# One more unit step between scores, turn and values in the attention loop of an attention and mixture-of-experts kernel

## The chip, the cores and the metric

The kernel runs on one core of one Trainium2 chip. The metric is the device time of one execution in microseconds. Three runs of the kernel before took 601.81, 603.10 and 607.35 us; their median is 603.1 us.

## The reference

Attention over q, k and v of shape (batch 8, heads 8, sequence 576, head dimension 64), all float32, and then a mixture of experts over the 4608 tokens of width 512 that the heads make together.

```python
rel = pos[:, None] - pos[None, :]
mask_local = (rel >= 0) & (rel < 32)
mask_strided = (rel >= 0) & (pos[None, :] % 32 == pos[:, None] % 32)
# heads 0 to 3 are local, heads 4 to 7 strided
scores = np.where(mask, scale * q @ k.T, -1e9)
attn = softmax(scores)              # denominator + 1e-09
x = (attn @ v), heads side by side  # 4608 x 512
logits = x @ w_gate + modality_bias[modality_id]
e_idx = argmax(logits); gate = softmax(logits)[e_idx]   # 8 experts
out = gate * (relu(x @ w1[e_idx]) @ w2[e_idx])          # 512 -> 1024 -> 512
```

## The kernel before, in words

**Two stages.** In the attention stage, up to about 165 us of the trace, the heads are computed and each token is routed to an expert. In the feed-forward stage that follows, 18 slots of 256 tokens of one expert each and a half slot of 128 tokens run one after the other, in three matmuls for each product (the float32 operands are split into a high and a low part).

**Units and steps.** The attention work is cut into 32 units, local and strided in turn. A local unit is one local head of two batches, a strided unit two strided heads of one batch. Eight units make a pair of batches. Each unit goes through `load` (queries and keys), `prep` (local only, copies of the queries into a block form), `masks` and `scores`, `load_values`, `turn` and `values`. The loop over `n` (lines 1050 to 1093) is a software pipeline: in step n it issues the scores of unit n, the turn of unit n-2 and the values of unit n-3. So in a local step (n even) the scores and the turn are of local units and the values of a strided one; in a strided step the other way round.

**What a unit computes.** `scores` multiplies queries and keys into two PSUM banks on TensorE (for a local unit L346, the tile `s`; for a strided one L442, `ss`), takes the maximum and the difference on VectorE (L353 and L354; L454 and L455) and the exponential on ScalarE (L355 and L356, tile `ex`; L456, tile `exs`). A strided unit is normalised here already: sum, +1e-9, reciprocal and product on VectorE (L458 to L462) give `en`. `turn` transposes on TensorE (the helper's line 227, tiles `t` and `ts`) and copies out of PSUM on ScalarE (L368 and L371 into `et`; L471 into `eb`). `values` multiplies by the values (L382 and L388, tile `o`; L483, tile `ot`). A local unit's result is normalised on VectorE (L392 to L398) into the rows `xt`, a strided unit's is copied on ScalarE (L491) into the columns `xc`.

**Buffers.** All PSUM tiles come from one pool of eight banks, used in turn; a step's masks, turn and values take two each. `ex` has two buffers (the pool's default) and `en` two fixed buffers that the units use in turn, with zeros in the last ten columns that GpSimd writes once at the start (L300). `et` has one buffer, the loaded tiles two.

**Order.** The order on TensorE is the program's (a manual schedule for that engine alone). The instructions of VectorE, ScalarE and GpSimd are put in order by a planner that simulates the program; those inside `pin` keep the program's order. The loads go out on SP's queue in program order. From step 3 on they are paced: the first half of the queries and keys of unit n+3 waits for the last values matmul, the second half for the last scores matmul, and the two parts of the values of unit n-1 for the last turn and the last values matmul (`follow`, L242). FILL puts matmuls on zeros ahead of the masks of steps 2 and 3.

**What hangs on the last values of a pair.** When the eighth unit's values are issued, a generator (`after`, L995) joins a list; every step takes five pieces from it. They turn the local rows into columns (tile `xl`), multiply by the gate weights (`lg`), turn the strided columns into rows (`xs`), rank the tokens by expert and, after the second, third and fourth pair, build the tables of slots. The rows are stored to memory by one DMA in each step on GpSimd's queue (`store_rows`). At steps nu-4, nu-3 and nu-2 (28, 29 and 30) the loop looks up, gathers and starts to load for the first two slots or halves of weights; at step nu+1 it turns the first slot's tokens. What is left of the last pair's list is done inside the first feed-forward slots.

Of the kernel before, what the change touches and what calls it, by code (L numbers as in the profile page):

```python
# [11 lines left out]
F32 = mybir.dt.float32  # L12
# [8 lines left out]
P = 128  # L21
# [170 lines left out]
def attention_moe(ctx: ExitStack, tc: tile.TileContext, a, out):  # L192
# [31 lines left out]
    at = {"scores": None, "turn": None, "values": None}  # L224
# [63 lines left out]
    lp = lp_cm.__enter__()  # L288


    def zeros(n, shape, name):
        return [lp.tile(shape, F32, bufs=1, name=f"{name}{i}") for i in range(n)]

    qds = zeros(2, [P, 18, 2, 32], "qd")
    ets = zeros(1, [P, 18, 2, 32], "et")
    ens = zeros(2, [P, 12, 64], "en")
    for t in qds + ets:
# [5 lines left out]
    class Local:  # L303
# [34 lines left out]
        def scores(self):  # L338
            n, qk, qd = self.n, self.qk, self.qd
            mx = lp.tile([P, 9], F32, tag="mx", name=f"mx{n}")  # L340
            self.ex = ex = lp.tile([P, 11, 64], F32, tag="ex", name=f"ex{n}")
            for g0, gn, s in self.ss:
# [60 lines left out]
    class Strided:  # L403
# [30 lines left out]
        def scores(self):  # L434
# [25 lines left out]
            nc.vector.reciprocal(sm[:], sm[:])  # L460
            self.en = ens[n % 2]
            nc.vector.tensor_tensor(self.en[:, :, 0:54], ex[:], bc(sm, 12), ALU.mult)  # L462
# [532 lines left out]
    def after(bp, xt, xcs):  # L995
        yield from finish_pair(bp, xt, xcs)
        yield
        for ph, (last_bp, _) in enumerate(PHASES):
            if bp == last_bp:
                yield from slots(ph)  # L1000
# [48 lines left out]
    man.__enter__()  # L1049
    for n in range(nu + 3):  # L1050
        paced = n >= PACED

        if not paced:
            for part in range(2):
                if n + 3 < nu:
                    units[n + 3].load(part, None)
            for part in range(2):
                if 1 <= n <= nu:
                    units[n - 1].load_values(part, None)
        if n in FILL:  # L1060
# [6 lines left out]
        if paced and n + 3 < nu:  # L1067
            units[n + 3].load(1, at["scores"])
        if 2 <= n <= nu + 1:
            units[n - 2].turn()  # L1070
        if paced and n <= nu:
            units[n - 1].load_values(0, at["turn"])
        if n >= 3:
            units[n - 3].values()
            if n - 3 in ends:
                extra.append(after(*ends[n - 3]))
        if paced and n <= nu:
            units[n - 1].load_values(1, at["values"])
        if n == SETUP:
# [5 lines left out]
        for i in range(2):  # L1085
# [4 lines left out]
            if n == nu - 2:  # L1090
                load(0, i)
        if n == nu + 1:
            turn(0)
# [70 lines left out]
```

## Time and profile before

| | before |
|---|---|
| median of three runs | 603.1 us (601.81 to 607.35) |
| profiled execution | 602.83 us |
| span of its trace | 601.0 us |
| TensorE busy | 565.7 us (94%) |
| VectorE busy | 446.8 us (74%) |
| ScalarE busy | 388.6 us (65%) |
| GpSimd busy | 250.4 us (42%) |
| granted clock of TensorE, mean | 0.993 |

The trace is of one execution. Its span starts with the first instruction and ends with the last; the run's time is 1.8 us longer. PE is TensorE, PEld its weight loads, DVE VectorE, ACT ScalarE, POOL GpSimd, SP the engine on whose queue the loads go out. A share of busy time over the whole span is a mean over the two stages, which differ: the feed-forward stage is two and a half times as long as the attention stage. "x<-y" names the tile written and the tiles read. A number in brackets after an instruction is the engine's idle time before it and what ended it; "issue" is idle time in which the engine waited for nothing that the profile shows. The clock is given as a share of full speed.

### The profile page before, as it was taken

How to read it: one execution, taken by the hardware profiler on the slowest of the kernel's cores; microseconds unless marked ns; L12 is line 12 of the kernel's file. 1: busy time of each engine (PE TensorE's matmuls, PEld its weight loads, DVE VectorE, ACT ScalarE, POOL GpSimd, SP SyncE). 2: the span in 40 equal slices, each digit the busy share in tenths (PEclk: the TensorE clock that was granted, in tenths of full speed). 3: DMA queues.
4: the chain of work that ended last, by engine and by line, in shares of the span. 5: the costliest groups of instructions: out<-in, count | busy, mean ns of one | idle time of the engine just before them, and what ended most of it. 6: DMA issues, size and time to landing. Idle time of an engine off the chain costs nothing.

```text
span 601.0 us, 15492 instructions
## 1 busy us (share of the span) xinstructions
PE 565.7 (94%) x6107; PEld 498.5 (83%) x6109; DVE 446.8 (74%) x1076; ACT 388.6 (65%) x798; POOL 250.4 (42%) x226
## 2 busy tenths in 40 slices
PE   8777899797899999999999999999999999999995
PEld 4666787676669999999999999999999999999994
DVE  7867886985968799666787787787787787787542
ACT  4767877765796666776665575575665665665652
POOL 0011011117237537555645645645645646532310
PEclk9999899999999999999999999999999999999998
DMA  8984997998844944744754743313214239413621
GB/s 311 299 259 152 335 316 257 322 306 273 267 115 164 219 168 105 217 170 106 177 210 106 219 167 93 71 36 105 72 37 106 70 116 277 111 40 72 228 103 41
DMA packets 73572, 102.46 MB, mean 170 GB/s; under 512 B 48531, under 2 KB 48787, under 8 KB 69908
## 3 DMA queue, kind: packets, MB, share of 16 engines
q0 software_dynamic: 20672, 58.01, 28.6%
q1 hardware_dynamic: 52340, 42.87, 26.8%
q8 instruction: 50, 0.82, 0.6%
q10 hardware_dynamic: 480, 0.51, 0.3%
q14 instruction: 30, 0.25, 0.1%
HBM read 123.85 MB, written 19.18 MB: 238 GB/s over the span
## 4 chain that ended last, share of the span: by engine, by line
PE 82%; ACT 7%; DVE 6%; issue 3%; POOL 0%; another core or an unknown queue 0%; POOLq 0%; ACTq 0%
PE h L940 34%; PE o L954 33%; PE o L382 2%; PE s L346 2%; PE ot L483 1%; ACT xc L491 1%; PE lg L543 1%; PE xs L227 1%; PE ts L227 1%; DVE ex L354 1%; DVE mx L353 1%; DVE sms L458 1%; PE t L227 1%; PE warm L212 1%; ACT et L368 1%
## 5 line engine op out<-in xcount | busy, mean ns | idle before, releaser
L976 DVE TENSOR_TENSOR wl<-raw,wh 128x512 fp32r<-128x512 f32 x288 | 187.7, 691 | 64.2 <-ACT wh L975 55.2
L975 ACT CAST wh<-raw 128x512 fp32r<-128x512 f32 x288 | 163.9, 619 | 66.6 <-PE o L954 43.1
L940 PE MATMUL h<-xh,wl 128*128 128x256 f32 x576 | 162.7, 283 | 0.0
L940 PE MATMUL h<-xl,wh 128*128 128x256 f32 x576 | 162.6, 283 | 0.0
L940 PE MATMUL h<-xh,wh 128*128 128x256 f32 x576 | 162.4, 282 | 0.1
L822 POOL DMA_INDIRECT raw<-in_w,wi x72 | 95.9, 1332 | 156.3 <-DVE wl L976 117.6
L940 PEld LDWEIGHTS h<-xh,wh 128*128 128x128 f32 x576 | 109.5, 190 | 7.5 <-issue 0.6
L940 PEld LDWEIGHTS h<-xl,wh 128*128 128x128 f32 x576 | 109.6, 190 | 5.5
L954 PE MATMUL o<-wh,hh 128*128 128x512 f32 x288 | 114.2, 396 | 0.0
L954 PE MATMUL o<-wl,hh 128*128 128x512 f32 x288 | 113.8, 395 | 0.0
L940 PEld LDWEIGHTS h<-xh,wl 128*128 128x128 f32 x576 | 109.7, 190 | 1.4 <-DVE wl L976 0.4
L954 PE MATMUL o<-wh,hl 128*128 128x512 f32 x288 | 110.5, 391 | 0.0
L943 ACT ACTIVATE hh<-h 128x256 fp32r<-128x256 f32 x144 | 55.4, 385 | 71.1 <-PE h L940 46.7
L945 DVE SCALAR_TENSOR_TENSOR hl<-h,hh 128x256 fp32r<-128x256 f32 x144 | 60.7, 421 | 33.3 <-ACT hh L943 21.6
L954 PEld LDWEIGHTS o<-wh,hl 128*128 128x128 f32 x288 | 53.5, 188 | 11.0
L954 PEld LDWEIGHTS o<-wh,hh 128*128 128x128 f32 x288 | 54.6, 189 | 7.6
L954 PEld LDWEIGHTS o<-wl,hh 128*128 128x128 f32 x288 | 54.6, 190 | 5.6
L962 POOL DMA_INDIRECT out<-y,le x36 | 44.7, 1242 | 20.6 <-ACT y L961 11.0
L806 POOL DMA_INDIRECT fx<-xd,le x36 | 40.1, 1113 | 11.9 <-issue 10.7
L813 POOL DMA_INDIRECT le<-ld,li x36 | 39.4, 1095 | 12.9 <-issue 10.1
L498 POOL DMA_DIRECT2D xd<-xt x20 | 14.5, 727 | 62.3 <-ACT xt L507 62.3
L382 PE MATMUL o<-vv,et 128*64 128x65 f32 x512 | 22.7, 231 | 5.5 <-issue 3.3
(189 smaller groups left out, 749.1 us busy)
## 6 DMA issues: line engine op xcount, KB each, us to landing
vv<-in_vl SPq DMA_DIRECT2D x32, 292.5 KB
qks<-in_qks SPq DMA_DIRECT2D x32, 288.0 KB
xd<-xt POOLq DMA_DIRECT2D x16, 512.0 KB
qk<-in_qkl SPq DMA_DIRECT2D x16, 304.0 KB
qk<-in_qkl SPq DMA_DIRECT2D x16, 288.0 KB
vs<-in_vs SPq DMA_DIRECT2D x32, 144.0 KB
raw<-in_w,wi POOLq DMA_INDIRECT x72
xd<-xt POOLq DMA_DIRECT2D x4, 256.0 KB
```

The source lines that it names most:

```text
L227: at["turn"] = nc.tensor.transpose(dst, src, ident)
L382: at["values"] = nc.tensor.matmul(o[64 * jj:64 * jj + 64, k, :], et[:, u, :, :].rearrange("p g q -> p (g q)"), vv[:, u, :], start=True, st ...
L806: pin(nc.gpsimd.indirect_dma_start(xt[:, h, :], None, xd[0:xrows, :], IOA(ap=le[:, h, 0:1], axis=0)))
L813: pin(nc.gpsimd.indirect_dma_start(le[:, h, :], None, ld[0:xrows, :], IOA(ap=li[:, s, h:h + 1], axis=0)))
L822: pin(nc.gpsimd.indirect_dma_start(raws[j].rearrange("p f c -> p (f c)"), None, a["w"], IOA(ap=wi[:, s, j:j + 1], axis=0), bounds_check=E ...
L940: nc.tensor.matmul(hp, w[:, a1], x[:, c, :], start=(k == 0), stop=(k == 11))
L943: nc.scalar.activation(hh[:], hp, AF.Relu)
L945: nc.vector.scalar_tensor_tensor(hl[:], hp, 0.0, hh.bitcast(F32), ALU.max, ALU.subtract)
L954: nc.tensor.matmul(os[h], hx[:, m], w[:, 512:1024], start=(f == 0 and i == 0), stop=(f == 7 and i == 2))
L962: outs.add(pin(nc.gpsimd.indirect_dma_start(out, IOA(ap=le[:, h, 0:1], axis=0), y[:], None, bounds_check=NT - 1, oob_is_err=False)))
L975: nc.scalar.copy(wh[:, c], raw[:, c])
L976: nc.vector.tensor_tensor(wl[:, c], raw[:, c], wh[:, c].bitcast(F32), ALU.subtract)
```

## The change

The turn of a unit is issued three steps behind its scores and its values four steps behind, in place of two and three. The value loads go out two steps behind the scores in place of one. The loop has one more pass, 36 in place of 35, and the list of a pair starts with the values of its last unit, so one step later. The steps at which slots are looked up, gathered and loaded keep their numbers; the turning of the first slot's tokens keeps its distance from the end. `ex` and `en` get a third buffer. Since the lag between scores and turn is now odd, a local step has local scores, a strided turn and local values, and a strided step has strided scores, a local turn and strided values.

```diff
--- before.py
+++ after.py
@@ -293,7 +293,7 @@
 
     qds = zeros(2, [P, 18, 2, 32], "qd")
     ets = zeros(1, [P, 18, 2, 32], "et")
-    ens = zeros(2, [P, 12, 64], "en")
+    ens = zeros(3, [P, 12, 64], "en")
     for t in qds + ets:
         nc.vector.memset(t[:], 0.0)
     for t in ens:
@@ -338,7 +338,7 @@
         def scores(self):
             n, qk, qd = self.n, self.qk, self.qd
             mx = lp.tile([P, 9], F32, tag="mx", name=f"mx{n}")
-            self.ex = ex = lp.tile([P, 11, 64], F32, tag="ex", name=f"ex{n}")
+            self.ex = ex = lp.tile([P, 11, 64], F32, tag="ex", bufs=3, name=f"ex{n}")
             for g0, gn, s in self.ss:
                 for g in range(gn):
                     for jj in range(2):
@@ -458,7 +458,7 @@
             nc.vector.tensor_reduce(sm[:], ex[:], AX.X, ALU.add)
             nc.vector.tensor_scalar(sm[:], sm[:], 1e-9, None, ALU.add)
             nc.vector.reciprocal(sm[:], sm[:])
-            self.en = ens[n % 2]
+            self.en = ens[n % 3]
             nc.vector.tensor_tensor(self.en[:, :, 0:54], ex[:], bc(sm, 12), ALU.mult)
 
         def turn(self):
@@ -1047,7 +1047,7 @@
             units[i].prep()
     man = tc.manual_schedule(engines={mybir.EngineType.PE})
     man.__enter__()
-    for n in range(nu + 3):
+    for n in range(nu + 4):
         paced = n >= PACED
 
         if not paced:
@@ -1055,8 +1055,8 @@
                 if n + 3 < nu:
                     units[n + 3].load(part, None)
             for part in range(2):
-                if 1 <= n <= nu:
-                    units[n - 1].load_values(part, None)
+                if 2 <= n <= nu + 1:
+                    units[n - 2].load_values(part, None)
         if n in FILL:
             keep_busy(FILL[n], f"warm{n}")
         if paced and n + 3 < nu:
@@ -1066,16 +1066,16 @@
             units[n].scores()
         if paced and n + 3 < nu:
             units[n + 3].load(1, at["scores"])
-        if 2 <= n <= nu + 1:
-            units[n - 2].turn()
-        if paced and n <= nu:
-            units[n - 1].load_values(0, at["turn"])
-        if n >= 3:
-            units[n - 3].values()
-            if n - 3 in ends:
-                extra.append(after(*ends[n - 3]))
-        if paced and n <= nu:
-            units[n - 1].load_values(1, at["values"])
+        if 3 <= n <= nu + 2:
+            units[n - 3].turn()
+        if paced and n <= nu + 1:
+            units[n - 2].load_values(0, at["turn"])
+        if n >= 4:
+            units[n - 4].values()
+            if n - 4 in ends:
+                extra.append(after(*ends[n - 4]))
+        if paced and n <= nu + 1:
+            units[n - 2].load_values(1, at["values"])
         if n == SETUP:
             routing_setup()
         if n + 2 < nu:
@@ -1089,7 +1089,7 @@
                 gather(i)
             if n == nu - 2:
                 load(0, i)
-        if n == nu + 1:
+        if n == nu + 2:
             turn(0)
     man.__exit__(None, None, None)
     lp_cm.__exit__(None, None, None)
```

## Rows read from the trace of the kernel before

**Rows 1.** Busy time by stage: stretch, length, us (instructions) per engine, clock, DMA, GB/s.

```profile
0.00:17.00 17.00, 14.48 (x232) 8.58 (x236) 12.97 (x29) 8.56 (x18) 0.54 (x6) 1.00 0.88 298
17.00:60.00 43.00, 33.48 (x901) 28.16 (x901) 31.39 (x85) 29.50 (x66) 4.33 (x8) 1.00 0.75 238
60.00:100.00 40.00, 36.02 (x956) 31.11 (x948) 31.64 (x105) 31.56 (x73) 4.83 (x8) 0.96 0.91 295
100.00:140.00 40.00, 32.88 (x810) 27.46 (x799) 33.25 (x133) 29.06 (x66) 9.52 (x11) 1.00 0.97 326
140.00:165.00 25.00, 20.19 (x472) 16.78 (x472) 20.01 (x85) 15.15 (x35) 11.14 (x14) 1.00 0.77 250
165.00:601.00 436.00, 428.68 (x2777) 386.40 (x2775) 317.53 (x642) 274.78 (x545) 220.07 (x181) 0.99 0.45 129
```

**Rows 2.** Waits of TensorE, 17 to 165 us: total us, times, longest.

```profile
PE ts L227 <- DVE en L462: 6.2, 5, 1.9
PE ot L483 <- issue: 3.6, 6, 0.9
PE o L382 <- issue: 3.3, 3, 2.3
PE xl L227 <- DVE xt L398: 1.9, 1, 1.9
PE o L382 <- ACT xc L514: 1.5, 2, 0.9
PE ot L483 <- ACT et L368: 1.3, 1, 1.3
PE ss L431 <- DVE xt L398: 1.0, 1, 1.0
```

**Rows 3.** Timeline of TensorE, turns that waited: start, us, what, [idle before].

```profile
22.53 0.85 PE L227 MATMUL ts<-cf_sb,en 128*128 128x128 f32 x6 [1.22 <-DVE en L462]
30.37 0.85 PE L227 MATMUL ts<-cf_sb,en 128*128 128x128 f32 x6 [1.94 <-DVE en L462]
71.22 1.54 PE L227 MATMUL ts<-cf_sb,en 128*128 128x128 f32 x6 [0.89 <-DVE en L462]
108.90 0.88 PE L227 MATMUL ts<-cf_sb,en 128*128 128x128 f32 x6 [1.47 <-DVE en L462]
152.57 0.87 PE L227 MATMUL ts<-cf_sb,en 128*128 128x128 f32 x6 [0.69 <-DVE en L462]
```

**Rows 4.** Busy time in one microsecond of the same kernel, columns as in group 1.

```profile
71.00:72.00 1.00, 0.78 (x4) 0.78 (x5) 0.97 (x8) 0.98 (x3) 0.00 (x0) 0.50 1.11 268
```

**Rows 5.** Waits of VectorE, 17 to 165 us, then its timeline and ScalarE's at 33.

```profile
DVE sms L458 <- ACT exs L456: 8.6, 8, 3.4
33.34 0.83 DVE L458 TENSOR_REDUCE sms<-exs 128x12 f32<-128x648 f32 x1 [1.51 <-ACT exs L456]
38.35 0.42 ACT L355 ACTIVATE ex<-ex 128x256 f32<-128x256 f32 x1 [5.04 <-DVE ex L354]
```

**Rows 6.** ScalarE's groups by shape, 30 to 160 us: count | busy us, mean ns.

```profile
L368 ACT COPY et<-t 64x512 f32<-64x512 f32 x26 | 15.0, 577 | 11.3 <-PE t L227 11.0
L491 ACT COPY xc<-ot 128x288 f32<-128x288 f32 x28 | 16.4, 684 | 3.4 <-PE lt L227 3.0
L456 ACT ACTIVATE exs<-exs 128x648 f32<-128x648 f32 x13 | 9.7, 746 | 3.4 <-DVE exs L455 3.3
L471 ACT COPY eb<-ts 128x512 f32<-128x512 f32 x13 | 7.7, 594 | 0.1
```

**Rows 7.** Waits of the SP queue, 20 to 165 us, and GpSimd's timeline at 125.

```profile
SPq L319 <- PE o L382: 12.7, 11, 3.1
125.46 1.10 POOL L822 DMA_INDIRECT raw<-in_w,wi  x1 [10.40 <-DVE wi L781]
```

**Rows 8.** Timeline of TensorE after the last scores, which end at 151.89 us.

```profile
151.13 0.76 PE L442 MATMUL ss<-qks 64*54 64x54 f32 x48
157.06 1.04 PE L483 MATMUL ot<-eb,vs 54*64 54x54 f32 x48 [1.25 <-ACT et L368]
```

## The prediction

> **What bounds the kernel now.** I read the busy time by stage first, because the edit touches only the loop over units. After 165 us, in the stretch of 436 us, TensorE is busy 428.7 [rows 1]: the feed-forward part is bound by TensorE, the edit has no instruction in it, and I take it as unchanged. The stake is the attention stage. From 17 to 165 us (148 us) TensorE is busy 33.48 + 36.02 + 32.88 + 20.19 = 122.6, VectorE 116.3, ScalarE 105.3 [rows 1]. Nothing is full over the whole stage, but single stretches are: from 100 to 140 us the DMA share is 0.97 and VectorE is busy 33.25 of 40; from 60 to 100 it is DMA 0.91 and TensorE 36.0 of 40. From 17 to 60 nothing is above 33.5 of 43. So from 17 to 60 time is lost to waiting for one another, and later mostly to full resources.
>
> Next, whom TensorE waits for in these 148 us. The largest item is the turn of a strided unit, which waits for the unit's normalised exponentials: 6.2 us in five waits [rows 2]. Line 470 reads `en`, written two steps after the scores started. The waits of "issue" (3.6 and 3.3 us) sit inside runs of value matmuls, where the profile shows nothing waited for; the edit leaves the number of these instructions alone, so they stay. The others are results of values (1.9 and 1.0), copies out of PSUM (1.5) and the copy of a turned local unit (1.3).
>
> **The change, term by term.** No arithmetic on TensorE, VectorE or ScalarE is added or removed. GpSimd clears one more small buffer in the first microseconds, where it works 0.54 us of 17 [rows 1]: nothing. The rest is order, and one extra pass of the loop.
>
> (1) The waits for `en`. With one more step between scores and turn, a whole step of TensorE's work lies in between, and I see no reason why the five waits should stay under that name. What is late next differs by place [rows 3]:
> - 1.22 us at 22.5 and 1.94 us at 30.4. Nothing is full from 17 to 60, but VectorE's queue had only just produced `en` in both cases, and its next evacuation of scores is behind it. Bounds 0 and 3.2; I take 2.4, nearer the upper end, since the stretch has the most idle time.
> - 0.89 us at 71.2 and 1.47 us at 108.9. Here the DMA share is 0.91 and 0.97 and VectorE works 33.25 of 40 in the second stretch. TensorE, let go earlier, meets the same VectorE queue one group later, at the banks of the scores, or meets the loads. Bounds 0 and 2.4; I take 0.
> - 0.69 us at 152.6: after it nothing is full. Bounds 0 and 0.7; I take 0.7.
>
> (2) The clock. In the microsecond from 71 to 72 the granted clock is 0.50, the lower level of 1.2 GHz [rows 4]. TensorE had idled before it (0.89 us of it stand in [rows 3]). The six turns there took 1.54 us against 0.88 at 108.9 [rows 3], so they lost 0.66, and the values behind them ran at the lower level too. If one of the idle times goes, the clock may stay up. Bounds: 0 and about twice 0.66, 1.3. I take 0.7.
>
> (3) The extra pass. The last scores end at 151.89 us; from there the loop only turns and takes values. Such a pass has little to hide a copy behind: at 157.06 the values waited 1.25 us for the copy of a turned unit [rows 8]. A further pass may cost such a wait again (+1.3); or it may gain, since one more unit's turn and values now lie between the last scores and their turn, and can cover that very wait (-1.3). I take +0.3. At the front, the first turns come a step later, scores a little earlier; filler matmuls stay in their steps. VectorE is busy 13.0 of the first 17 us with the DMA share at 0.88 [rows 1], so the work there arrives no faster: 0.
>
> (4) What shares a step. Types alternate, so a shift by one swaps partners. Before, a local step carries local scores, the local turn and strided values; a strided step the rest. After, a local step has local scores, a strided turn and local values; a strided step has strided scores, a local turn and strided values. For ScalarE, the two large copies of a local turn (2 x 0.577) and the two of strided values (2 x 0.684) leave the local step, which had the local exponentials too, and join the strided step with its exponential of 0.746; the `eb` copies (0.594 for the larger) go the other way [rows 6]. The load is more even, but the exponential on which VectorE's sum waits now stands beside 2.5 us of copies. As the order on ScalarE and VectorE is drawn up by the planner, the bounds are -7 (rival C) and +10 (rival D). I take 0.
>
> (5) DMA queues. Every value load (two issues for a local unit, four for a strided one) moves one step on, and its use too; its distance to use stays two steps. On SP's queue it now follows a query-key load of the other type, and waits for the same kinds of TensorE instruction. SP waited 12.7 us in all in eleven value loads of local units for values matmuls [rows 7], with the scores' loads queued behind; TensorE's pace sets that wait, and it remains. Bounds: -0.5 and +0.5, 0 taken. On POOL's queue the stores of a finished pair's rows come one step later, while the lookups, gathers and first weight loads stay at their step numbers. The tables also come a step later: the first weight load, which waited 10.4 us and went at 125.46 [rows 7], would go near 130. It is needed at 165, so 35 us of cover shrink to 30: 0. If that cover were gone, the load's delay of about 5 us would be paid in full. The turning of the first slot's tokens moves with the last pass but one: 0.
>
> Sum: -2.4 - 0 - 0.7 - 0.7 + 0.3 = -3.5 us. The profiled execution took 602.83 us (span 601.0, so 1.8 lie around it), 0.3 under the median of 603.1. 602.83 - 3.5 = 599.3; I say **599.3 us**.
>
> **The forecast's own range.** With all of the lower bounds in (1) to (3), -3.2 - 2.4 - 0.7 - 1.3 - 1.3 = -8.9: 593.9. With all of the upper ones, +1.3: 604.1. Both at once are unlikely; 595 to 603 is its own range. Chance 0.48.
>
> **Rival B: the wait changes its name and nothing is gained.** Eight PSUM banks go round, and a step takes six of them before the routing's own; so TensorE can be little more than a step ahead of the copies, whatever the lag. VectorE's evacuation of the next scores stands ahead of or right behind `en` in one queue, so the wait would return at the banks. For it: the full stretches of [rows 1], and bank waits exist already (1.5 and 1.0 in [rows 2]). Against it: 2.5 times as much is named for `en`. It gives 602.83 plus (3), about 603; 601 to 605. Chance 0.23. By the Trainium skill ("Perfetto Trace Analysis", Optimization Strategy), the same gap coming back again and again on the engine that should be full can mean too little room in SBUF or PSUM for the next tile. By that rule, read for PSUM, the time is this rival's 603; read for SBUF, the third buffer would serve. The trace speaks for neither alone, since the gaps on `en` are five and of uneven size.
>
> **Rival C: the even steps free all waits on copies.** The local step's backlog on ScalarE is what let it starve later: it sat idle 5.04 us before 38.35 while VectorE had waited 1.51 us for it at 33.3 [rows 5]. If the swap of (4) breaks this ping-pong, the waits of [rows 2] on results go: 6.2 + 1.9 + 1.5 + 1.3 + 1.0 = 11.9, and 1.3 of the clock: 13.2 us, 589.6. Against: 60 to 140 us is near full. With half of it lost there, 596. So 588 to 597. Chance 0.15.
>
> **Rival D: slower, by the queue order in the strided step.** VectorE's sum waited for the strided exponential 8.6 us in eight waits already [rows 5]. If the planner puts that exponential behind the four copies that now share its step, it comes 2 x 0.577 + 2 x 0.684 - 0.594 = 1.9 us later in each of 16 strided units: up to 30 us of VectorE standing still, with the next scores' evacuation behind it. VectorE has 31.7 us to spare in 148. TensorE feels it through the banks. It decides if more than a third, 10 us, reaches TensorE: 602.83 + 10 - 3.5 = 609.3; I put the rival at 610, 606 to 614. Against: the copies of the turn are ready about when the maximum and the difference on VectorE still run, so they fill a gap before the exponential, and the local step leaves no backlog any more. Chance 0.14.
>
> That the change doesn't do what it says I rule out: the steps are written out for TensorE by hand.
>
> **Chances and range.** A measurement of this kernel can tell about 1% from no change: 597.1 to 609.1. Faster: C nearly whole (0.14) and a third of the forecast (0.16): 0.30. Slower: most of D, 0.11, and 0.02 for an unforeseen delay of the first weights: 0.13. Within 1%: 0.57. Range 592 to 607: it drops the better half of C (0.07) and the worse part of D (0.10).
>
> **What would show it.** The turns of strided units no longer wait for `en`, and what waits in their place is the values or the scores' masks, on banks. The end of the attention stage moves from 165 to about 162 us; the length behind it stays within 1 us of 436. The clock holds 1.00 from 71 to 74. ScalarE's idle time before the local exponentials (5.04) shortens in C; the 8.6 us of VectorE's sum grow past 15 in D. The forecast is wrong if TensorE's waits from 17 to 165 us change by more than 9 us in sum, or if the feed-forward part changes its length.

## The result and the profile after

The changed kernel took 607.8 us (median of 20 runs, 605.9 to 611.92), the kernel before on the same chip 604.72 us (20 runs, 601.81 to 609.8). The ratio is 1.0056, with a 95% interval from 1.0036 to 1.0075: slower by about 3 us, where 3.5 us less were forecast, and 0.8 us outside the range. Executions over 1.5% above the fastest of the same kernel stand in the medians and are left out of the ratios, so that a ratio below can differ from the quotient of two medians. The profiled execution of the changed kernel took 607.72 us, its span is 605.9 us.

The busy time by stage answers to [rows 1]; the columns are the same. After 165 us the stretch is longer because the feed-forward part starts later.

```profile
17.00:60.00 43.00, 38.93 (x1017) 32.26 (x1016) 34.10 (x93) 34.39 (x78) 4.37 (x8) 1.00 0.84 269
60.00:100.00 40.00, 36.00 (x866) 30.43 (x866) 31.77 (x103) 29.55 (x70) 5.01 (x8) 0.91 0.85 279
100.00:140.00 40.00, 31.96 (x683) 24.98 (x677) 29.71 (x126) 23.81 (x55) 9.10 (x11) 0.91 0.86 287
140.00:165.00 25.00, 20.05 (x430) 16.49 (x430) 15.79 (x64) 14.18 (x34) 9.77 (x12) 0.86 0.70 228
```

From 17 to 60 us TensorE does 38.93 us of work where it did 33.48: the lead that was forecast is there, and larger. From 100 to 140 us it runs 683 matmuls where it ran 810, and from 60 us on the granted clock stands at 0.91 and 0.86 where it was 0.96 to 1.00. Both are losses.

The balance up to the first feed-forward matmul, in the kernel before and then in the changed one:

```profile
0.00:165.62 165.62, 137.58 (x3336) 112.39 (x3338) 129.87 (x442) 114.45 (x256) 30.37 (x45) 0.99 0.86 282
0.00:170.24 170.24, 146.24 (x3338) 117.12 (x3338) 129.47 (x449) 113.01 (x256) 29.94 (x46) 0.94 0.83 274
```

TensorE's idle time fell from 28.0 to 24.0 us. Its busy time rose by 8.7 us for the same matmuls, at a mean clock of 0.94 against 0.99. An estimate from these two clocks: about 20 us at the lower level of 0.50 after, about 3 before; at half speed the difference costs up to 8.6 us. So in these two executions the gain is there, and by this estimate the slower clock takes back twice as much. But the profiled execution of the kernel before is not a usual one: its clock over the whole run, 0.993, was reached by only 11 of the 157 executions of that kernel in the runs below (medians of 0.981 to 0.987 by chip), and it is 1.9 us under the median of 604.72. How much of the 3 us between the medians is clock can't be read from two traces.

The waits of TensorE from 17 to 165 us (total us, times, longest) answer to [rows 2].

```profile
PE o L382 <- issue: 3.7, 9, 0.9
PE s L346 <- issue: 2.4, 5, 1.0
PE ss L442 <- issue: 2.3, 3, 1.5
PE en L639 <- POOL hv L633: 2.3, 1, 2.3
PE xl L227 <- DVE exs L455: 1.9, 3, 0.8
PE s L334 <- DVE exs L455: 1.6, 2, 1.1
```

The 6.2 us for `en` are gone. What is late next is small for the most part (masks and turned rows behind VectorE's exponentials). The list is now led by "issue", in values matmuls (L382) and in scores (L346, L442), and by one wait of 2.3 us for GpSimd's `hv` near the end of the stage.

Where the lead went is read from first instructions of a kind, in us. The last column is the same changed kernel in run e15 (chip E, below); its profiled execution is the quickest of its twelve.

| first instruction of | before | after | after, in e15 |
|---|---|---|---|
| first pair's logits (L543) | 54.14 | 50.20 | 51.44 |
| second pair's table of entries (L639) | 114.73 | 113.24 | 112.81 |
| third pair's logits (L543) | 131.25 | 135.85 | 129.41 |
| third pair's table of entries (L639) | 158.03 | 161.34 | 151.63 |
| feed-forward part (L940) | 165.62 | 170.24 | 158.58 |

In the changed kernel each of the first four comes behind one more unit's scores (1.2 us and masks), so its lead is a little more than the difference. The lead of 3.9 us at the first logits has shrunk to 1.5 us by 113 us, and at 136 us the changed kernel is 4.6 us behind. The timeline of TensorE in that place (start, us, instructions, idle before them):

```profile
126.69 0.88 PE L227 MATMUL ts<-cf_sb,en 128*128 128x128 f32 x6
127.49 0.52 PE L382 MATMUL o<-vv,et 128*64 128x65 f32 x6
128.41 0.35 PE L382 MATMUL o<-vv,et 128*64 128x65 f32 x4 [0.40 <-issue]
129.15 0.39 PE L382 MATMUL o<-vv,et 128*64 128x65 f32 x5 [0.38 <-issue]
...
132.73 0.50 PE L382 MATMUL o<-vv,et 128*64 128x65 f32 x3 [0.91 <-issue]
133.45 0.27 PE L382 MATMUL o<-vv,et 128*64 128x65 f32 x1 [0.22 <-issue]
134.17 0.49 PE L382 MATMUL o<-vv,et 128*64 128x65 f32 x3 [0.45 <-issue]
134.60 1.33 PE L227 MATMUL xl<-cf_sb,xt 128*128 128x128 f32 x5
135.85 2.67 PE L543 MATMUL lg<-xc,rt_sb 128*32 128x256 f32 x32
```

36 values matmuls take 7.1 us, in pieces of a few with a gap before each, one about every 0.72 us. Then the five turns behind them take 1.33 us and the logits 2.67, against 0.76 and 1.93 in the kernel before: the granted clock is 0.50 from 132 to 136 us (shown below). GpSimd at the same time, in the changed kernel:

```profile
125.63 1.09 POOL L822 DMA_INDIRECT raw<-in_w,wi  x1 [11.52 <-DVE tk L798]
127.03 1.02 POOL L822 DMA_INDIRECT raw<-in_w,wi  x1 [0.31 <-DMA vs<-in_vs]
128.35 0.98 POOL L813 DMA_INDIRECT le<-ld,li  x1 [0.30 <-DVE en L462]
129.63 0.96 POOL L813 DMA_INDIRECT le<-ld,li  x1 [0.30 <-issue]
130.90 0.94 POOL L813 DMA_INDIRECT le<-ld,li  x1 [0.30 <-issue]
132.15 0.94 POOL L813 DMA_INDIRECT le<-ld,li  x1 [0.30 <-issue]
140.74 0.76 POOL L498 DMA_DIRECT2D xd<-xt  x1 [7.64 <-ACT xt L507]
```

and in the kernel before, behind the load that [rows 7] shows:

```profile
126.86 1.39 POOL L822 DMA_INDIRECT raw<-in_w,wi  x1 [0.30 <-issue]
135.40 0.77 POOL L498 DMA_DIRECT2D xd<-xt  x1 [7.15 <-ACT xt L507]
136.47 1.03 POOL L813 DMA_INDIRECT le<-ld,li  x1 [0.31 <-DVE mx L353]
```

Before, the four lookups (L813) stand behind the third pair's first row store in GpSimd's queue, and that store holds them back until 136. After, the pair's list begins a step later, the lookups keep their step, and so they pass the store and follow the two weight loads without a pause: six indirect DMAs in a row from 125.6 to 133.1. That they and TensorE's gaps belong together is what the experiments test.

### The profile page after: what moved, and what is told of

Same layout as the page of the kernel before. It is cut to its first block, busy times and chain, and to the rows that moved or that the text cites. A ratio compares the mean times of both kernels' runs of the same rounds, so it can differ in the third digit from the quotient of the medians.

```text
span 605.9 us, 15511 instructions
## 1 busy us (share of the span) xinstructions
PE 574.4 (95%) x6109; PEld 503.2 (83%) x6109; DVE 446.4 (74%) x1076; ACT 389.2 (64%) x798; POOL 243.9 (40%) x227
## 4 chain that ended last, share of the span: by engine, by line
PE 77%; DVE 14%; ACT 4%; issue 3%; DMA 1%; POOL 1%; POOLq 0%; SPq 0%; ACTq 0%
PE h L940 34%; PE o L954 33%; DVE sms L458 2%; DVE ex L354 1%; DVE mxs L454 1%; DVE en L462 1%; DVE mx L353 1%; PE o L382 1%; DVE xt L398 1%; PE s L346 1%; DVE exs L455 1%; ACT exs L456 1%; PE xs L227 1%; PE lg L543 1%; PE ts L227 1%
## 5 line engine op out<-in xcount | busy, mean ns | idle before, releaser
L940 PE MATMUL h<-xh,wl 128*128 128x256 f32 x576 | 162.7, 283 | 0.0
L940 PE MATMUL h<-xl,wh 128*128 128x256 f32 x576 | 162.6, 283 | 0.0
L940 PE MATMUL h<-xh,wh 128*128 128x256 f32 x576 | 162.4, 282 | 0.1
L822 POOL DMA_INDIRECT raw<-in_w,wi x72 | 89.4, 1241 | 163.1 <-DVE wl L976 125.3
L940 PEld LDWEIGHTS h<-xh,wh 128*128 128x128 f32 x576 | 109.5, 190 | 7.5 <-issue 0.6
L940 PEld LDWEIGHTS h<-xl,wh 128*128 128x128 f32 x576 | 109.6, 190 | 5.5
L940 PEld LDWEIGHTS h<-xh,wl 128*128 128x128 f32 x576 | 109.6, 190 | 1.4 <-DVE rt L760 0.4
L806 POOL DMA_INDIRECT fx<-xd,le x36 | 40.4, 1123 | 11.0 <-issue 11.0
L813 POOL DMA_INDIRECT le<-ld,li x36 | 39.3, 1091 | 12.8 <-issue 10.1
L382 PE MATMUL o<-vv,et 128*64 128x65 f32 x512 | 24.5, 234 | 4.0 <-issue 3.7
```

The costliest lines, as they stand in the source:

```text
L382: at["values"] = nc.tensor.matmul(o[64 * jj:64 * jj + 64, k, :], et[:, u, :, :].rearrange("p g q -> p (g q)"), vv[:, u, :], start=True, st ...
L806: pin(nc.gpsimd.indirect_dma_start(xt[:, h, :], None, xd[0:xrows, :], IOA(ap=le[:, h, 0:1], axis=0)))
L813: pin(nc.gpsimd.indirect_dma_start(le[:, h, :], None, ld[0:xrows, :], IOA(ap=li[:, s, h:h + 1], axis=0)))
L822: pin(nc.gpsimd.indirect_dma_start(raws[j].rearrange("p f c -> p (f c)"), None, a["w"], IOA(ap=wi[:, s, j:j + 1], axis=0), bounds_check=E ...
L940: nc.tensor.matmul(hp, w[:, a1], x[:, c, :], start=(k == 0), stop=(k == 11))
```

## Experiments

The runs below were taken in five groups on five chips, named A to E here; a ratio is always to runs of the kernel before in the same group. The unedited changed kernel was measured in the result, whose chip isn't on record, and on E, but not on A to D. The median of the kernel before was 605.32, 605.41, 604.95, 599.75 and 599.6 us on A to E. "Gaps" below are the idle times of TensorE put down to issue, from 115 to 165 us of the profiled execution, that lie within 0.75 us of one of GpSimd's indirect DMAs: 4.25 us in 10 in the kernel before, 4.86 us in 12 in the changed one. Single idle times of the same kind lie elsewhere in every profile, those of chip E too; they are not counted.

**e1, chip A: the lookups put back behind the store.** The changed kernel with

```diff
-            if n == nu - 4:
+            if n == nu - 3:
                 look_up(i)
```

and the gathers and first loads one step later as well (nu - 2, nu - 1).

> The changed kernel, with the lookup, gather and first weight load of the first two slots one unit step later each, so that they stand behind the third pair's first row store on GpSimd's queue again, as in the kernel before. Theory A (the lag pays in the attention stage, and the loss comes from the lookups, which kept their step numbers and now fall into the first weight loads): TensorE's values group at 127 to 134 us, which took 7.1 us, shortens to 2 to 3 us, the clock stays up there, and the time falls by 4 to 6 us against the changed kernel, to 602 to 604 beside about 604.5 of the kernel before. Theory B (the deeper pipeline itself costs the time, by bank waits and the extra pass): within 1.5 us of the changed kernel, 606 to 609.

Measured: 606.39 us, ratio 1.0026 (0.9996 to 1.0055). The order on GpSimd's queue is the old one, and the third pair's logits start at 129.45 us. But lookups, stores and gathers now follow one another from 135.5 to 147.5 us, and the scores in that stretch are cut up in their place:

```profile
139.78 0.50 PE L346 MATMUL s<-qk,qd 128*64 128x64 f32 x4 [0.31 <-issue]
140.52 0.27 PE L346 MATMUL s<-qk,qd 128*64 128x64 f32 x1 [0.23 <-issue]
...
145.69 0.74 PE L346 MATMUL s<-qk,qd 128*64 128x64 f32 x9 [0.93 <-issue]
```

36 score matmuls took 6.6 us, against 1.2 undisturbed. So moving the lookups moves the gaps more than it ends them; whether it gives back a part of the loss, the interval doesn't tell.

**e2, chip A: the lookups put ahead of the store in the kernel before.** Lookups, gathers and first loads at nu - 5, nu - 4, nu - 3; nothing else is changed.

> The kernel before (old lags), with the lookup, gather and first weight load one unit step earlier, so that the lookups stand ahead of the third pair's first row store on GpSimd's queue, as in the changed kernel. Theory A: the matmuls near 128 us stall as in the changed kernel, and the time rises by 4 to 6 us, to 608 to 611 beside about 604.5. Theory B: no difference from the kernel before, within 1.5 us.

Measured: 607.74 us, ratio 1.0048 (1.0021 to 1.0076), with GpSimd's four lookups from 127.78 to 132.54 us right behind the loads. TensorE's timeline shows the picture of the changed kernel, with the old lag:

```profile
128.34 0.28 PE L442 MATMUL ss<-qks 64*36 64x36 f32 x4 [0.47 <-issue]
129.07 0.28 PE L442 MATMUL ss<-qks 64*36 64x36 f32 x4 [0.46 <-issue]
...
132.06 0.52 PE L382 MATMUL o<-vv,et 128*64 128x65 f32 x5 [0.26 <-issue]
134.90 1.33 PE L227 MATMUL xl<-cf_sb,xt 128*128 128x128 f32 x5
```

The third pair's logits start at 136.16 us, 4.9 later than in the kernel before. So the earlier place of lookups, gathers and first loads makes by itself a loss of the size of the change's. It doesn't do so by the sum of the gaps, which is 4.27 us against 4.25. But in e2 eight idle times put down to issue (3.0 us) lie close together between 126 and 134 us, and the clock is low behind them. The stretch from 130 to 137 us, in the kernel before and then in e2:

```profile
130.00:137.00 7.00, 7.00 (x129) 5.47 (x128) 4.72 (x13) 4.04 (x9) 1.30 (x2) 1.00 0.96 360
130.00:137.00 7.00, 6.07 (x54) 4.24 (x57) 2.94 (x9) 2.33 (x5) 1.93 (x3) 0.51 0.88 323
```

**e3, chip A: the wait for `hv`.** The changed kernel, with the third pair's table of entries taken five list items later (L635):

```diff
-        for _ in range(LW):
+        for _ in range(LW + 5 * (bp == 2)):
```

> The changed kernel, with the last matmuls of the third pair's ranking (those of line 639) issued five list pieces later, a step later on TensorE. If the wait of 2.3 us for GpSimd's product near 161 us and the lower clock behind it (the matmuls took 2.1 us in place of 1.2) are a cost of the extra pass, the time falls by 2 to 3.5 us against the changed kernel, to 604 to 606. If that wait is hidden (the scores of the last unit bound the tail in any case), it stays within 1 us of the changed kernel's 607.8.

Measured: 607.73 us, ratio 1.0038 (1.0011 to 1.0065). The wait is gone from its profile, and no gain can be told; the unedited changed kernel wasn't run beside it.

**e4, chip A: two buffers in place of three.** The changed kernel with two `en`, two `ex`, and `ens[n % 2]`.

> The changed kernel with two buffers for the exponentials (ex and en) in place of three. A strided unit's exponentials are written at its own step and read three steps later, and the next unit but one of its type writes the same buffer four steps later, so the second buffer should do: within 1.5 us of the changed kernel's 607.8. If VectorE works far behind TensorE, the product into the buffer waits for the turn and the time rises by 2 us or more.

Measured: 610.76 us, ratio 1.0099 (1.0064 to 1.0133), missed: the other two changed kernels on this chip stood at 1.0026 and 1.0038, so the third buffers are worth about 0.6 to 0.7%, near 4 us. Where, one profile doesn't show: its first logits come at 52.75 us against 50.20, but so do those of e5 below, which has the third buffers.

**e5 and e6, chip B: the longer lag in the early steps only.** `BACK` is 17 in e5 and 25 in e6:

```diff
-        if 3 <= n <= nu + 2:
-            units[n - 3].turn()
+        for i in range(n - 3 if n <= BACK else n - 2, n - 2 if n < BACK else n - 1):
+            if 0 <= i < nu:
+                units[i].turn()
...
```

and the like for the values (one step later) and their loads. In both, the local unit at the step back takes its values with the exponentials of the next local unit.

> The longer lag is kept up to unit step 17; there two units are turned, one step later two units' values are taken, and from then on turns and values stand two and three steps behind the scores, as in the kernel before, with three buffers throughout. So the second pair's list, the tables, the loads, the lookups and the stores go back to the steps and the queue order of the kernel before, and the extra pass is gone. Theory (the gain of the longer lag is made before 60 us, the loss after 100 us, through what the later lists do to GpSimd's queue and the tail): the lead at the first logits stays and the loss is not made: 599 to 602 us, faster than before by 0.5 to 1%. Rival 1 (the lead is worth nothing, since the stretch from 60 to 140 us is bound by DMA): 603 to 606, the same as before. Rival 2 (what costs is the lag itself in the early steps, by the swapped partners): at or above 606.

> As the kernel in which the lag goes back at step 17, but it goes back at step 25, just ahead of the end of the third pair. The tables of the first experts come a step later, as in the changed kernel; the third pair's list, the row stores and the tail are at their old steps. Theory (loss by the third pair's list, the stores' place in GpSimd's queue and the extra pass): 599 to 603 us. Rival (the later second list and the later tables, with the first weight loads, also cost): 3 us more than the kernel with the step at 17. If the lag itself costs in the middle, from 60 to 140 us: above 605.

Measured: e5 603.3 us, ratio 0.996 (0.9926 to 0.9994); e6 606.04 us, ratio 1.0016 (0.9989 to 1.0043). e5 is faster than the kernel before by 2 us: its ratio is below 1, though its median lies in the window of the first rival, and e6 is 2.7 us above e5, as its rival had it. The lag in the early steps is a gain; what the steps from 17 to 25 add is a loss. In e6 the lookups stand behind the store, as in the kernel before (134.16 us, the store at 133.09), so this loss is not that of their place. Whether it is the second list, the tables and loads that hang on it, or the lag itself in the middle (e6 is above 605), isn't settled by these two.

**e7 and e8, chip B: half of the lookups left out.** Into the changed kernel (e7) and the kernel before (e8):

```diff
-        if k < len(plan) and plan[k][1] in tables:
+        if k == 1:
+            found[1] = found[0]
+        elif k < len(plan) and plan[k][1] in tables:
```

and the like in `gather`.

> The changed kernel, but the second slot takes the entries and token rows of the first: its two lookups and two gathers of token rows are left out, so half of GpSimd's indirect DMAs (two of the four lookups and two of the four gathers) near the end of the attention stage are gone, and the second slot's rows of the output are the first's. Theory (an indirect DMA that GpSimd issues leaves TensorE short of instructions for about its own 0.95 to 1.25 us, and the clock falls after it): four of them gone give back 2 to 4 us, 604 to 606, and the run of values matmuls at about 127 us takes 3 to 4 us in place of 7.1. Rival (the gaps of TensorE there come from elsewhere, the stores or the value loads): within 1 us of the changed kernel.

> The kernel before with the same four indirect DMAs left out (the second slot takes the first slot's entries and rows). If TensorE's gaps come with them there too: 1.5 to 3 us below the kernel before, about 602, and the gaps between 137 and 148 us halve. Against the changed kernel with them left out it shows whether the change still costs with half of the lookups: if the lookups were the whole loss, the two agree within 1.5 us; if the extra pass and the tail cost as well, the changed one is still 1.5 to 3 us above.

Measured: e7 603.01 us, ratio 0.9937 (0.9903 to 0.9972); e8 601.03 us, ratio 0.9929 (0.989 to 0.9967). Four DMAs of about a microsecond of issue each, off TensorE's path, are worth 4.4 us in the kernel before. With them gone the two kernels agree by their ratios; by the medians the changed one is still 2 us above, so whether the lookups were the whole loss isn't settled. The gaps fell to 2.81 us in 7 and 2.07 us in 5, and in e7 the values matmuls that took 7.1 us took 4.6, with two lookups behind the loads in place of four.

**e9 and e10, chip C: the lookups spread over three steps**, in the changed kernel and in the kernel before. In e9:

```diff
-            if n == nu - 4:
+            if n == nu - 3 + i:
                 look_up(i)
-            if n == nu - 3:
+            if n == nu - 2 + i:
                 gather(i)
```

> The changed kernel, with the lookups and gathers of the first two slots spread over three steps: the first slot's lookup one step later than in the changed kernel, then the second's lookup with the first's gather, then the second's gather, so that at most four of GpSimd's indirect DMAs stand back to back, with row stores between. Theory (long chains of indirect DMA issues starve TensorE, short ones do not): TensorE's runs of values matmuls no longer take over 3 us there, 600 to 604 us, at or below the kernel before. Rival 1 (each indirect DMA costs its own time, wherever it stands): within 1.5 us of the kernel with both lookups one step later, 606. Rival 2 (the second slot's gather comes after the ranking's product and its tokens are late for the feed-forward part): the span from the first feed-forward matmul grows by over 1 us.

> The kernel before with the same spreading, one unit step earlier than in the changed kernel. Theory: its own two chains (gaps of about 5 us in TensorE between 137 and 149 us) shrink to half: 601 to 604. Rival (each indirect DMA costs its own time wherever it stands): the same as the kernel before, 605.

Measured: e9 603.68 us, ratio 0.9966 (0.993 to 1.0003); e10 604.62 us, ratio 0.9989 (0.9954 to 1.0024). In the kernel before, the spreading is worth nothing that can be told, and its gaps (5.44 us in 13) did not shrink. The changed kernel comes to the kernel before, with gaps of 2.82 us in 8.

**e11, chip C: early lag and spread lookups together.** e5 with the spreading, and with the local unit's values taken ahead of the next local turn at the step back.

> The longer lag up to unit step 17 only, then the old distances, with the spreading of the lookups; at the step back the values of the local unit are taken ahead of the next local unit's turn. If the gain of the early lag (2 us in the kernel that went back at 17) and the gain of the spreading add up: 599 to 602, below both kernels. If the spreading is worth nothing: 603. If the gain of the early lag was an accident of that measurement: as the kernel before with the spreading.

Measured: 601.67 us, ratio 0.9955 (0.9922 to 0.9988). It beats the kernel before, but by no more than e5 does, and its gaps are 5.34 us in 12, more than before: nothing of the gain is put down to the spreading.

**e12, e13, e14 and e16: plain DMAs in place of the eight indirect ones.** In the changed kernel (e12 on chip C, e14 on D, e16 on E) and in the kernel before (e13 on D):

```diff
-            pin(nc.gpsimd.indirect_dma_start(le[:, h, :], None, ld[0:xrows, :], IOA(ap=li[:, s, h:h + 1], axis=0)))
+            pin(nc.gpsimd.dma_start(le[:, h, :], ld[P * h:P * h + P, :]) if n in ("0_0", "0_1") else ...)
```

and the like for the token rows (L806).

> The changed kernel, but the eight indirect DMAs of the first two slots' lookups and gathers are plain DMAs of the same size from fixed rows on the same GpSimd queue, so the entries and tokens of these two slots are not the chosen ones. Theory (what starves TensorE is the indirect form, with its descriptors made on GpSimd): 600 to 603, and no gaps of TensorE beside the plain ones; the two first weight loads, still indirect, keep theirs. Rival (it is the data of these transfers, or any DMA that GpSimd issues): within 1.5 us of the changed kernel, 607.

> The kernel before with the eight indirect DMAs of the first two slots' lookups and gathers as plain DMAs of the same size from fixed rows, so the entries and tokens of these two slots are not the chosen ones. If the longer lag has a gain of its own that only the indirect DMAs had eaten: this stands 2 to 4 us above the changed kernel with the same edit, at 602 to 604. If the longer lag is worth nothing even without them: the two agree within 1 us, at about 600, and the kernel before had paid some 5 us for these eight DMAs itself.

> The changed kernel with the eight plain DMAs once more, on the same chip and beside the same runs as the kernel before with that edit, since 2 us between the two can only be told side by side: 599 to 601 by its earlier run.

> The changed kernel with the eight plain DMAs, beside the unedited one. Theory (the indirect DMAs make the loss): 5 to 9 us below the unedited changed kernel and at or below the kernel before. If the two are within 2 us, the earlier difference was one between chips, and the theory falls.

Measured: e12 599.81 us, ratio 0.9914 (0.9882 to 0.9946); e13 600.02 us, ratio 0.9972 (0.9933 to 1.0011); e14 600.11 us, ratio 1.0001 (0.9969 to 1.0033); e16 600.53 us, ratio 0.9999 (0.9971 to 1.0027). The time of the changed kernel with plain DMAs is the same on three chips, to 0.8 us. It is the kernel before that differs, 605 or 600. On chip C the gaps fell to 0.78 us in 2, both beside the two weight loads, which are still indirect; beside the plain ones there are none. But in e12 these don't stand in the place of the indirect ones. With nothing to look up first, they went earlier:

```profile
115.25 2.15 POOL L813 DMA_DIRECT2D le<-ld  x4
137.32 2.20 POOL L806 DMA_DIRECT2D fx<-xd  x4
```

The lookups stand at 115 us in place of 128 and no longer beside the dense values matmuls, so e12 changes form, place and length at once. In e13 the plain ones do stand in the old place, behind the store at 134.48 us, but on D there are no gaps at all beside GpSimd's DMAs, not even beside the weight loads, which are indirect. There the two kernels agree, and e13 says nothing on what the kernel before pays on the other chips.

**e15, e17 and e18, chip E: the changed kernel itself, and e9 and e11 again, side by side.** No edits beyond those shown.

> The changed kernel itself, unedited, on the chip and beside the runs of the next three, so that they can be compared with it and not only with the kernel before. By its first measurement 0.4 to 0.8% above the kernel before.

> The changed kernel with its lookups and gathers spread, beside the unedited one: by the theory 3 to 5 us below it, at the kernel before or 1 to 2 us below.

> The longer lag up to step 17 only, with the spread lookups, once more: if it does beat both kernels, 0.2 to 0.8% below the kernel before and over 1% below the changed one on this chip too.

Measured: e15 597.34 us, ratio 0.9966 (0.9934 to 0.9998); e17 598.02 us, ratio 0.9975 (0.9947 to 1.0003); e18 596.03 us, ratio 0.9957 (0.9929 to 0.9984). On this chip the unedited change is faster than the kernel before, by 2 us, and the expectations of e15, e16 and e17 fell: neither spreading nor plain DMAs help, the plain ones cost 3.2 us, and no run shows why. GpSimd in e15, the same lookups in the same place:

```profile
127.91 0.97 POOL L813 DMA_INDIRECT le<-ld,li  x1 [0.30 <-DVE mx L353]
129.18 0.96 POOL L813 DMA_INDIRECT le<-ld,li  x1 [0.30 <-issue]
130.45 0.94 POOL L813 DMA_INDIRECT le<-ld,li  x1 [0.30 <-issue]
131.70 0.94 POOL L813 DMA_INDIRECT le<-ld,li  x1 [0.30 <-issue]
```

and TensorE in e15 beside them:

```profile
126.24 0.88 PE L227 MATMUL ts<-cf_sb,en 128*128 128x128 f32 x6
127.05 0.69 PE L382 MATMUL o<-vv,et 128*64 128x65 f32 x16
...
128.10 0.68 PE L382 MATMUL o<-vv,et 128*64 128x65 f32 x15
128.71 0.77 PE L227 MATMUL xl<-cf_sb,xt 128*128 128x128 f32 x5
129.41 2.38 PE L543 MATMUL lg<-xc,rt_sb 128*32 128x256 f32 x30
```

The values take 1.66 us where the profiled execution of the result took 7.1. The gaps beside the thirteen indirect DMAs of e15 sum to 0.00 us. The stretches from 127 to 132 and from 132 to 136 us, in the changed kernel of the result and then in e15 (columns as in [rows 1]):

```profile
127.00:132.00 5.00, 3.13 (x35) 2.20 (x33) 2.40 (x7) 1.93 (x5) 3.91 (x4) 0.86 0.86 298
132.00:136.00 4.00, 2.60 (x16) 1.68 (x19) 1.70 (x7) 1.91 (x5) 0.94 (x1) 0.50 0.91 312
```

```profile
127.00:132.00 5.00, 4.80 (x83) 3.21 (x81) 3.78 (x11) 3.57 (x9) 3.78 (x5) 1.00 0.96 358
132.00:136.00 4.00, 4.00 (x123) 3.42 (x118) 1.46 (x4) 2.86 (x6) 1.40 (x2) 1.00 0.89 344
```

35 matmuls against 83, 16 against 123, and a clock of 0.50, the lower level of 1.2 GHz, here only where TensorE had been cut up. By the table above, the two executions of one program are 0.4 us apart in time at the second table of entries, 6.4 at the third logits, 9.7 at the third table and 11.7 at the feed-forward part; their medians are 10.5 us apart. So most of what sets the result apart from e15 arises behind 113 us, and it is not in the program alone. No profile of the unedited kernel before was taken beside the runs on D and E, so whether it had gaps there isn't shown.

## Why the prediction was wrong

**Step (1), the waits for `en`: right.** The waits left the list, masks and results took their place, and third buffers were needed (e4). The forecast was -3.1 for (1), and TensorE's idle time up to the feed-forward part fell by 4.0 us. The lead of 3.9 us at the first logits is in the program: in the profiles of kernels that have the longer lag there they come at 49.99 to 52.75 us, in those with the old lag at 53.09 to 55.07. As a gain in time it shows in e5, e11 and e18 (0.4 to 0.45%), where the lag goes back at step 17, and in the unedited change on chip E (-2.0 us, 0.1 to 4.0 by the interval).

**Step (2), the clock: wrong, and it is the term of the sum that the profile contradicts most.** It put -0.7, for a clock that falls less. In the two profiled executions the clock was lower for longer: TensorE's busy time rose by 8.7 us, and by the estimate above the clock makes up to 8.6 of them. The microsecond from 71 to 72 still has a clock of 0.50 (before: [rows 4]), and from 65 to 70 it is 0.57, with waits of 0.67 and 1.14 us just before and in it. From 132 to 136 us a stretch at 0.50 was added. No term of the working allowed for a clock that falls more often. The trace of the kernel before has an unusually high clock, which makes the step look worse here, and which had shown the prediction a single lower stretch.

**Step (3), the extra pass: 0.3 us were put, and it is not settled.** The tail waited 2.3 us for `hv` in the result, 1.2 us in e15. e3, which takes this wait away, shows no gain.

**Step (4), the swapped partners: nothing speaks against the 0.** VectorE's sum waited 10.3 us for the strided exponentials in 12 waits, against 8.6 in 8 [rows 5]; rival D asked for more than 15. No run has the swap alone.

**Step (5), the queues: this is the step that failed, as it left out what cuts up TensorE's work behind 115 us.** It saw that the stores move one step on while "the lookups, gathers and first weight loads stay at their step numbers", and put 0 after asking only whether the data comes in time. It comes in time; the first weight load, put near 130, went at 125.63, and its cover, counted as 35 us shrinking to 30, was 40 by the working's own 125.46 and 165. What it left out is what GpSimd's queue does to TensorE: with the store gone from ahead of them, the lookups join the weight loads. e2 makes the same move in the kernel before and loses 0.48%; e7 and e8 take half of these DMAs out and are 0.6 and 0.7% faster than the kernel before. So the move makes a loss of the right size on A, and such DMAs cost as much on B. That it is the whole loss is not shown: e1, with the lookups behind the store again, stands between the two kernels, and e6 loses 2.7 us against e5 without that move.

**The sign of it stood in the trace of before, though hardly in the line that the prediction read.** [Rows 2] has 3.6 and 3.3 us of "issue" in values matmuls, and the text let them stand, because "the edit leaves the number of these instructions alone". Of these 6.9 us only 1.2 lie beside an indirect DMA on GpSimd, and the longest, 2.30 us at 120.46, does not. But after 115 us scores and turns have such idle times as well; of 6.55 us in all, 4.25 lie beside an indirect DMA, among them:

```profile
128.29 0.33 PE L442 MATMUL ss<-qks 64*36 64x36 f32 x9 [0.52 <-issue]
138.49 0.28 PE L483 MATMUL ot<-eb,vs 36*64 36x36 f32 x3 [0.45 <-issue]
139.22 0.32 PE L483 MATMUL ot<-eb,vs 36*64 36x36 f32 x3 [0.45 <-issue]
147.56 1.16 PE L346 MATMUL s<-qk,qd 128*64 128x64 f32 x31 [0.50 <-issue]
```

An idle time with no releaser has a cause all the same; laid beside the other engines' timelines it would have given one more rival: the lookups beside a dense run of small matmuls, and a slower clock behind it. Its size could not have been read there, since the sum of the gaps grew only to 4.86 us.

**What the runs show, and what stays open.** Shown: gaps of TensorE beside indirect DMAs of GpSimd (2.07 to 5.68 us in the eleven profiles of kernels with indirect lookups on A, B and C), and none in the changed kernel on chip E (e18 has 1.66 us in 2 there); that the earlier place of the lookups costs about 3 us on A (e2), and that leaving half of them out gains about 4 on B. The sum of the gaps doesn't rank the kernels: e2 has no more than the kernel before and is slower, e10 has 5.44 us and is not. Where the gaps are gone, the change is 2 us faster on E; on D, with plain DMAs and no gaps, the two kernels agree (e13, e14), so a gain of the whole change has been seen on one chip only. Open: whether it is the indirect form that makes the gaps, or the place and length of the chain, since e12 changed all three; what the steps from 17 to 25 add; and what differs between the chips, or between the times at which they ran. The lookups take 0.94 to 0.98 us of GpSimd in the result and in e15; neither the queues' totals nor the order of instructions tell the two apart. Nor is it shown by what way GpSimd's work reaches TensorE. By the Trainium skill ("DMA: Bandwidth & Descriptors", section "SWDGE vs HWDGE vs iDMA") software on GpSimd makes the descriptors of its DMAs, plain and indirect alike. No run here shows who makes them; in GpSimd's time the runs tell the two apart (four plain lookups took 2.15 us in e12, the four indirect ones 4.74 in the changed kernel).

**The chances.** Within 1% was put at 0.57, and 0.56% it was, but on the other side and for a reason that no rival had, so that is luck. The range missed because nothing but rival D reached above 605. A part of the miss is its base: it starts from 603.1, the median of three executions, and twenty gave 604.72; 603.1 times 1.0056 is 606.5, inside the range. The sign would have been wrong all the same.

## What to carry to other kernels

When a step is moved, ask of every queue not only whether its data still comes in time, but which work now stands back to back, and what runs on TensorE beside it. Idle time that the profile puts down to issue should be laid beside the other engines' timelines before it is called fixed. A change of half a per cent can have one sign on one chip and the other on the next: e11's order, with the longer lag in the early steps only, was 0.4% faster than the kernel before on C and on E, and is the one to keep, though on E it can't be told from the change itself (0.9957 against 0.9966).

## What the runs showed of the hardware that was not expected

While GpSimd issued indirect DMAs back to back, TensorE got its matmuls in pieces of 1 to 9, about every 0.72 us, in the result and in runs on chips A, B and C, and in the changed kernel of the result its clock was 0.50 from 132 to 136 us. The same program in e15, on chip E, had none of this, and was 10.5 us (1.7%) faster by the medians; of the 12.2 us between the spans of the two profiles, 11.2 arise between 113 us and the first feed-forward matmul. The feed-forward part, with nearly all of the 72 indirect loads of weights, kept its length: 435.4 us before, 435.7 after, 435.1 in e15.
